# A channel stage in two passes, token mixing by split operands, and an order written as a list

## The chip, the cores and the metric

One core of a Trainium2 chip. Its engines run their own instruction queues in order: TensorE (PE) multiplies matrices into 8 PSUM banks, VectorE (DVE), ScalarE (ACT) and GpSimd (POOL) work on tiles of 128 partitions, and SyncE (SP) starts transfers. Engines wait for each other through semaphores. The metric is the device time of one execution in microseconds; smaller is better. A profiled execution also has a span, from its first instruction to its last.

## The reference

Three stages follow one another: a recurrent attention with gates (2 sequences, 8 heads, 768 steps, width 40), a causal attention with 4 experts of which each token takes 2, and a mixer, first over the tokens, then over the channels. All in float32.

```python
for t in range(S):                                   # first stage
    m_new = np.maximum(f_gate[:, :, t] + m, i_gate[:, :, t])
    f_stab = np.exp(f_gate[:, :, t] + m - m_new)
    i_stab = np.exp(i_gate[:, :, t] - m_new)
    C = f_stab * C + i_stab * einsum('bhd,bhe->bhde', vt, kt)
    n = f_stab * n + i_stab * kt
    y[:, :, t] = sigmoid(o_gate[:, :, t]) * (C q) / max(|n q|, 1)
...
for e in range(E):                                   # second stage, x = y, width 320
    a = softmax(causal(scale * (x @ wq[e]) @ (x @ wk[e]).T))
    out += weight_of_expert_e * (a @ (x @ wv[e]) @ wo[e])
...
xt = x.transpose(0, 2, 1)                            # third stage
h = np.maximum(xt @ w_tok1, 0.0) @ w_tok2            # 768 -> 256 -> 768
u = x + h.transpose(0, 2, 1)
h2 = np.maximum(u @ w_ch1, 0.0) @ w_ch2              # 320 -> 1536 -> 320
return u + h2
```

## The kernel before

**Tiles and stages.** The 2 x 768 tokens are 12 row chunks of 128, (b, i) with b the sequence and i from 0 to 5. The first stage goes chunk by chunk (the functions `m_...`, tiles `vs`, `w`, `e`, `cc`, `cb`, `dc`, `dn`, `x`): inside a chunk as an attention with decays, between chunks by a state `cc`. `p_qk`, `p_v` and `p_rank` make queries, keys, values and the choice of experts (`q`, `ks`, `vg`); `a_scores`, `a_unit`, `a_value`, `a_scale` and `a_tail` are the second attention (`am`, `atr`, `c`, `yh`), and `a_tail` (L1023) leaves its output, a product with `wo`, as rows `u`. `t_hidden` (L1056) and `t_mix` (L1078) mix the tokens: `t_hidden` needs all six chunks of a sequence and gives `ht`, `t_mix` adds to `u`, chunk by chunk. `c_turn` (L1100) transposes u to `ut`, `c_hidden` (L1118) and `c_out` (L1135) are the channel products, `c_store` (L1150) adds the result to u and stores it.

**Precision.** Most products are split: an operand is a hi tile in the type fp32r and a lo tile, the rest; a product is hi·hi + hi·lo + lo·hi, three matmuls. The first token product is the exception: one matmul in fp32 per chunk and half, with the weight `tw` and the rows `u` unsplit (L1062).

**Weights of the mixer** come as 64-bit words and are turned into float32 by `narrow` (L543): ACT scales the upper halves (L556), DVE shifts (L559), puts the lower halves' bits in (L561), and the sign (L564), ACT makes hi (L571), DVE or POOL lo (L302). This is called conversion below. The channel weights are 12 blocks k (`cw`), each with a first (`c1`, 384 columns) and a second part (`c2`, 320). A block needs a home in SBUF: three have their own, others get what the first two stages leave, and the last five (`PAGED`) take large buffers.

**Channel stage.** For each of three groups g of four chunks, all 12 blocks are gone through: `c_hidden(k, g)` gives h (ACT hi, DVE lo L1131), `c_out(k, g)` adds into four PSUM banks, which stay taken over the 12 blocks. Then `c_store` adds each to u, on DVE, and stores.

**Order.** The engines' queues are filled by `Plan` (L81). Each part of the work is a generator, whose steps name the engines that may run them (A, V, G for ACT, DVE, POOL; W is DVE for a step that is not planned beside one of POOL), an assumed cost, what must be done first, and the buffers taken. The planner takes, step by step, what can start first by its assumed times (`LAG`, costs), ties going by `RANK`, and gives the step to the engine that it thinks earliest. Where PE would be idle, it puts filler matmuls on a constant tile (`fillers`, L307, tile `still`) until 46 us of planned time.

Of the kernel before, what the change touches and what calls it, by code (L numbers as in the profile page):

```python
# [12 lines left out]
F32 = mybir.dt.float32  # L13
# [21 lines left out]
PAGED = 5  # L35
# [5 lines left out]
FILL = 46.0  # L41
LAG = {f: {"P": p, "A": a, "V": v, "G": g, "S": x} for f, p, a, v, g, x in (
    ("P", 0.0, 0.2, 0.2, 0.24, 0.2), ("A", 0.17, 0.0, 0.12, 0.155, 0.15), ("V", 0.17, 0.12, 0.0, 0.155, 0.15),
    ("G", 0.13, 0.09, 0.09, 0.0, 0.12), ("S", 0.1, 0.1, 0.1, 0.1, 0.0), ("", 0.0, 0.0, 0.0, 0.0, 0.0))}
DEP = 0.115
TURN = 0.11
WINDOW = 3.4133
WARM = 6.85
ARRIVE = 1.7
RATE = 405.0  # L50
LATE = (11.0, 1.7), (22.0, 2.4), (0, 0.8)
DEEP = 8
COSTLY = {"V": 1.2, "G": 1.2}
PAT = {"P": 0.004, "A": 0.004, "V": 0.004, "G": 0.004, "S": 0.004}


RANK = [
# [23 lines left out]
class Plan:  # L81


    def __init__(self, free, pool, lands, fill):
        self.free = dict(free)
        self.pool = {t: [(0.0, "")] * n for t, n in pool.items()}
        self.events, self.counts = {}, {}
        self.live, self.waiting = [], {}
        self.now, self.eng, self.order = 0.0, "", 0
        self.mode, self.act, self.win, self.cold = "F", {}, 0, False  # L90
        self.port = 0.0
        self.lands = list(lands)
        self.fill, self.filling = fill, True

    def add(self, part):
        self.order += 1
        p = [(RANK[self.order - 1], self.order), part, None, 0.0, ""]
        self.resume(p)

    def resume(self, p):  # L100
        try:
            p[2] = next(p[1])
        except StopIteration:
            return
        self.park(p)

    def park(self, p):
        for k in p[2][1]:
            if k not in self.events:
                self.waiting.setdefault(k, []).append(p)  # L110
                return
        self.live.append(p)

    def mark(self, key, lag=0.0):
        self.events[key] = (self.now + lag, self.eng if not lag else "")
        for p in self.waiting.pop(key, []):
            self.park(p)
# [9 lines left out]
    def give(self, tag, n=1, lag=0.0):  # L127
        self.pool.setdefault(tag, []).extend([(self.now + lag, self.eng)] * n)

    def landed(self, kb):  # L130

        t = max(self.lands[-1], self.now + ARRIVE) + kb / RATE
        self.lands.append(t)
        return t + next(x for z, x in LATE if t < z or z == 0) * (kb > 100 or t < LATE[1][0]) - self.now

    def start(self, p):
        opts, after, take, keep, mode, _, dmas = p[2]
        deps = [(p[3], p[4])] + [self.events[k] for k in after]
        for tag, n in take:
            have = self.pool.get(tag, [])  # L140
            if len(have) < n + (keep.get(tag, 0) if isinstance(keep, dict) else keep):
                return None
            deps += sorted(have)[:n]
        best = None
        for o, cost in opts:
            e = "V" if o == "W" else o
            s = max([self.free[e], self.port if o in "WG" else 0.0] + [t + (LAG[f][e] if f != e else 0.0 if e in "PS" else DEP) for t, f in deps])
            if dmas:
                s = max(s, self.lands[dmas - 1 - DEEP] - 0.65 * (dmas - 1))
            if e == "P" and mode != self.mode:  # L150
                s += TURN
            if best is None or s + cost * COSTLY.get(e, 1.0) < best[0] + best[2] * COSTLY.get(best[1], 1.0):
                best = (s, e, cost)
        return best

    def clock(self, t):

        while (self.win + 1) * WINDOW <= t:
            last, full = [self.act.get(w, 0.0) / WINDOW for w in (self.win - 1, self.win)]
            self.cold = full < 0.44 if self.cold else full < 0.36 and last < 0.45  # L160
            self.win += 1
        return 1.91 if self.cold or t < WARM else 1.0

    def stream(self, s, cost, duty):
        long = cost * self.clock(s)
        t, end = s, s + long
        while t < end - 1e-9:
            w = int(t / WINDOW + 1e-9)
            z = min(end, (w + 1) * WINDOW)
            self.act[w] = self.act.get(w, 0.0) + (z - t) / long * cost * duty  # L170
            t = z
        return long

    def still(self, s):

        if not self.filling:
            return
        if s > FILL:
            self.filling = False
            self.give("bank")  # L180
            return
        n = 0
        while self.free["P"] + 0.17 < s:
            self.free["P"] += self.stream(self.free["P"], 0.056, 0.95)
            n += 1
        if n:
            self.fill(n)

    def run(self):
        while self.live:  # L190
            cand = {}
            for p in self.live:
                c = self.start(p)
                if c:
                    cand.setdefault(c[1], []).append((c[0], p, c[2]))
            if not cand:
                raise RuntimeError("no part can go on: %s" % [(p[0], p[1].__name__, p[2]) for p in self.live])
            pick = None
            for e, cs in cand.items():
                s0 = min(c[0] for c in cs)  # L200
                c = min((c for c in cs if c[0] <= s0 + PAT[e]), key=lambda c: c[1][0])
                if c[0] > s0 + 0.004:
                    fits = [x for x in cs if x[0] + x[2] <= c[0] + 0.03]
                    c = min(fits, key=lambda c: c[1][0]) if fits else c
# [21 lines left out]
def on(opts, *after, take=(), keep=0, mode="F", duty=0.9, dmas=0):  # L226
    opts = (opts,) if isinstance(opts[0], str) else opts
    t = {}
    for x in take:
        t[x] = t.get(x, 0) + 1  # L230
# [1081 lines left out]
```

## Time and profile before

| what | value |
|---|---|
| median of 3 runs | 338.07 us (337.53 to 338.20) |
| the profiled execution | 338.06 us |
| its span | 336.3 us |
| busy: PE, DVE, ACT, POOL | 327.9, 232.5, 176.5, 37.2 us |
| chain that ended last | 69% PE, 24% DVE |
| granted TensorE clock | 1.00 |

The table is read from the bottom: the clock is at its full value throughout, so a matmul has the same price everywhere. PE's 97% is a share of the whole span, in which filler matmuls and stretches paced by other engines count as busy, so the chain says more: what ended last was PE in most of the span and DVE in a part. Where these parts lie is to be seen in the rows below.

### The profile page before, as it was taken

The page shows a single profiled execution, that of the slowest core. Times are in us where ns is not written, and L with a number is a line of the kernel's source. Part 1 is how long each engine was busy: PE and PEld are TensorE (multiplying, and loading weights), DVE is VectorE, ACT ScalarE, POOL GpSimd, SP SyncE. Part 2 cuts the span into 40 slices and gives each one's busy share as a digit, 9 for nine tenths or more (in the row PEclk, how much of TensorE's full clock was granted, in tenths as well). Part 3 has the DMA queues.
Part 4 walks back from the last instruction along what each step waited for, and adds up shares of the span by engine and source line. Part 5 has one row for each costly group of instructions (what it writes and reads, how often), then busy time and mean ns, then how long its engine had stood idle before and what let it go on. Part 6 is the DMA issues. An engine that isn't in the chain of part 4 may idle for free.

```text
span 336.3 us, 7705 instructions
## 1 busy us (share of the span) xinstructions
PE 327.9 (97%) x3049; PEld 293.6 (87%) x3049; DVE 232.5 (69%) x662; ACT 176.5 (52%) x435; POOL 37.2 (11%) x65
## 2 busy tenths in 40 slices
PE   7899999999999999999999999999999999999995
PEld 6689999898998889888888898999999889898985
DVE  5999999999999799999878656996231122411113
ACT  4785797848578779776876634453111121211110
POOL 4311133241212010010201100000000000000000
PEclk9999999999999999999999999999999999999999
DMA  7973443633500367010002502200020000200002
GB/s 215 415 287 102 161 164 116 239 106 106 176 29 2 119 182 253 12 64 24 2 0 89 173 0 88 86 1 3 0 78 2 0 2 0 78 2 0 0 2 78
DMA packets 10300, 29.05 MB, mean 86 GB/s; under 512 B 1272, under 2 KB 3224, under 8 KB 10264
## 3 DMA queue, kind: packets, MB, share of 16 engines
q1 hardware_dynamic: 10120, 28.54, 24.6%
q8 instruction: 24, 0.39, 0.5%
q14 instruction: 12, 0.10, 0.1%
q10 hardware_dynamic: 144, 0.02, 0.0%
HBM read 26.50 MB, written 1.97 MB: 85 GB/s over the span
## 4 chain that ended last, share of the span: by engine, by line
PE 69%; DVE 24%; ACT 3%; issue 2%; DMA 1%; SPq 0%; DVEq 0%; ACTq 0%
PE bank L278 63%; PE bank L976 3%; DVE am L959 2%; DVE tf L561 2%; DVE e L681 2%; DVE tf L564 2%; DVE cw L302 1%; DVE w L305 1%; DVE tf L559 1%; PE bank L719 1%; ACT am L965 1%; DVE xt L771 1%; DVE vs L305 1%; DVE c L1026 1%; DMA gt<-in_dram 1%
## 5 line engine op out<-in xcount | busy, mean ns | idle before, releaser
L1131 DVE SCALAR_TENSOR_TENSOR h<-bank,h 128x512 fp32r<-128x512 f32 x36 | 24.8, 690 | 75.2 <-ACT h L1129 75.2
L278 PE MATMUL bank<-ut,cw 128*128 128x512 f32 x288 | 70.9, 395 | 0.0
L278 PE MATMUL bank<-cw,h 128*128 128x320 f32 x432 | 68.0, 310 | 0.0
L1129 ACT ACTIVATE h<-bank 128x512 fp32r<-128x512 f32 x36 | 21.5, 597 | 86.1 <-PE bank L278 86.1
L278 PEld LDWEIGHTS bank<-cw,h 128*128 128x128 f32 x432 | 65.0, 188 | 1.7
L278 PEld LDWEIGHTS bank<-ut,cw 128*128 128x128 f32 x288 | 53.0, 188 | 10.8 <-issue 0.2
L965 ACT ACTIVATE am<-am,mn 128x128 f32<-128x128 f32 (+5 forms) x48 | 32.1, 670 | 9.1 <-DVE mn L962 5.0
L959 DVE CUSTOM_DVE_ANT_0 am<-bank,mk 128x384 f32<-128x384 f32 (+3 forms) x64 | 30.5, 498 | 3.2 <-PE bank L278 2.8
L278 PE MATMUL bank<-xt,wh 128*128 128x256 f32 x144 | 25.7, 286 | 0.4 <-DVE e L681 0.4
L976 PE MATMUL bank<-ident,am 128*128 128x128 f32 x168 | 23.4, 275 | 0.3 <-ACT dn L746 0.2
L278 PEld LDWEIGHTS bank<-xt,wh 128*128 128x128 f32 x144 | 21.4, 188 | 1.3 <-DVE e L681 0.6
L299 ACT COPY atr<-bank 128x384 f32<-128x384 f32 (+3 forms) x51 | 20.7, 453 | 2.1 <-PE bank L976 1.7
L278 PE MATMUL bank<-atr,vg 128*64 128x128 f32 x336 | 21.6, 277 | 0.0
L556 ACT ACTIVATE tf<-raw 128x384 f32<-128x384 f32 (+1 forms) x32 | 17.2, 540 | 8.4 <-DVE cw L302 7.0
L976 PEld LDWEIGHTS bank<-ident,am 128*128 128x128 f32 x168 | 19.3, 140 | 2.3 <-ACT dn L746 0.5
L278 PE MATMUL bank<-ks,q 64*128 64x384 f32 (+2 forms) x192 | 20.9, 341 | 0.0
L278 PEld LDWEIGHTS bank<-atr,vg 128*64 128x64 f32 x336 | 18.3, 137 | 2.2 <-issue 0.4
L278 PEld LDWEIGHTS bank<-ks,q 64*128 64x128 f32 x192 | 15.2, 184 | 3.6 <-issue 1.2
L561 DVE SCALAR_TENSOR_TENSOR tf<-raw,tf 128x384 uint32<-128x384 uint32 (+1 forms) x32 | 16.6, 526 | 0.3
L564 DVE SCALAR_TENSOR_TENSOR tf<-raw,minus,tf 128x384 uint32<-128x384 uint32 (+1 forms) x28 | 16.1, 582 | 0.2
L681 DVE TENSOR_TENSOR e<-bank,e 128x512 f32<-128x512 f32 x24 | 16.0, 678 | 0.0
L571 ACT CAST cw<-tf 128x320 fp32r<-128x320 f32 (+1 forms) x24 | 11.7, 486 | 8.0 <-DVE tf L564 7.9
(165 smaller groups left out, 582.2 us busy)
## 6 DMA issues: line engine op xcount, KB each, us to landing
kv<-in_dram SPq DMA_DIRECT2D x11, 848.0 KB
raw<-in_dram SPq DMA_DIRECT2D x20, 384.0 KB
raw<-in_dram SPq DMA_DIRECT2D x13, 320.0 KB
os<-in_dram SPq DMA_DIRECT2D x4, 480.0 KB
out_dram<-u SPq DMA_DIRECT2D x12, 160.0 KB
raw<-in_dram SPq DMA_DIRECT2D x3, 386.0 KB
kv<-in_dram SPq DMA_DIRECT2D x1, 512.0 KB
gt<-in_dram SPq DMA_DIRECT2D x1, 512.0 KB
```

Of the source, the lines that this page charges most:

```text
L278: PE.matmul(o, lt, r, start=first, stop=last)
L299: (A.copy if e == "A" else V.tensor_copy)(o, i)
L556: A.activation(t, w[:, :, 1].bitcast(F32), AF.Copy, scale=2.0 ** -112)
L561: V.scalar_tensor_tensor(u, w[:, :, 0], 29, u, op0=OP.logical_shift_right, op1=OP.bitwise_or)
L564: V.scalar_tensor_tensor((hi if lo is None else t).bitcast(U32), w[:, :, 1], minus.bitcast(U32), u, op0=OP.bitwise_and, op1=OP.bitwise_or)
L571: A.copy(hi, t)
L681: V.tensor_mul(EE[n, u], PS[n][u], EE[n, u])
L959: V.tensor_tensor_reduce(a[:, b0 * 128:b1 * 128], s["p", e, ci], mks, -0.125, 3e38, OP.add, OP.min, s["mn"][:, ci, e:e + 1])
L965: A.activation(a[:, 0:w], a[:, 0:w], AF.Exp, bias=s["mn"][:, z, e:e + 1], scale=-1.0, accum_out=s["sm"][:, 0, e:e + 1])
L976: PE.transpose(pt[:, k - b0], a[:, k * 128:(k + 1) * 128], ident)
L1129: A.activation(h[0], p1, AF.Relu)
L1131: V.scalar_tensor_tensor(h[1], p1, 0.0, f32(h[0]), op0=OP.max, op1=OP.subtract)
```

## The change

**Order.** The planner goes: `ORDER` lists every step, x // 5 being the part and x % 5 the engine ("PAVGS"); a negative number is so many fillers (80 in all, 119 before), and `STOP` gives their bank back. Costs and keeps disappear from the code.

**Engines.** Several steps lose the choice of POOL: the w product of `m_carry`, the lo parts of the weights of the second attention and of wo, of the converted weights, the gates, the output gate's scaling.

**Token mixing.** `tw(0)` is split like the other weights, `a_tail` makes hi and lo tiles `up` of its output, and `t_hidden` has three matmuls per chunk and half.

**Channel stage.** Two passes h of six blocks each, and in each pass the three groups. Results are added to u after each pass, and stored after the second. Blocks of the first pass give their homes back when all three groups have used them (`room`); no block takes large buffers.

```diff
-PAGED = 5
+HALF = NK // 2
...
+        for x in ORDER:
+            if x == STOP:
+                self.give("bank")
+            elif x < 0:
+                self.fill(-x)
+            else:
+                self.step(self.parts[x // 5], "PAVGS"[x % 5])
...
     def m_carry(n):
...
-        yield on((pool(512), dve2(512)), ("kv", n))
+        yield on("V", ("kv", n))
         mul(plan.eng, w, w, KQ[n % KVB][:, 4:8])
...
     def out_weights():
...
-        yield on((dve2(640), pool(640)))
+        yield on("V")
         sub(plan.eng, WO[1], raw, f32(WO[0]))
...
     def narrow(src, n, home, rem, after, done):
...
-        if lo is None:
-            give("tf")
-            count(done, 4)
-            return
-        yield on(act(n))
+        yield on("A")
         A.copy(hi, t)
-        yield on((("G", (0.2 if rem else 0.1) + n / 435.0), ("W", 0.73 if rem else dve2(n)[1])))
+        yield on("V")
...
     def token_home(n):
-        TW[n] = [big([128, 4, 384], F32R if n else F32, "tw") for _ in range(n + 1)]
+        TW[n] = [big([128, 4, 384], F32R, "tw") for _ in range(2)]
...
     def a_tail(b, i):
...
         copy(plan.eng, uo(b, i), px)
-        give("bank")
         mark(("u0", b, i))
+        yield on("AV", take=["big"] * (1 - i % 2))
+        if i % 2 == 0:
+            UP[b, i // 2] = big([128, 2, 2, DM], F32R, "up")
+        hi, lo = [UP[b, i // 2][:, x, i % 2] for x in range(2)]
+        copy(plan.eng, hi, px)
+        yield on("V")
+        V.tensor_sub(lo, px, f32(hi))
+        give("bank")
+        mark(("up", b, i))
...
     def t_hidden(b, m):
...
-            mm(ph, tw(0, 0)[:, m0:m0 + 128], uo(b, c), c == 0, c == NCH - 1)
+            for k, (w, x) in enumerate(((0, 0), (0, 1), (1, 0))):
+                mm(ph, tw(0, w)[:, m0:m0 + 128], UP[b, c // 2][:, x, c % 2], c + k == 0, c == NCH - 1 and k == 2)
...
     def c_out(k, g):
         for i in range(4):
+            new = k % HALF == 0
...
+            if new and i == 0:
+                ACC[k // HALF, g] = [bank([128, DM]) for _ in range(4)]
...
+            if (k + 1) % HALF == 0:
+                mark(("done", k // HALF, 4 * g + i))
...
+        if k < HALF:
+            plan.tally(("cwused", k), 3, lambda: room(*HOME[k]))
...
+    def c_store(h, n):
+        yield on("V", ("done", h, n), *((("sp", n),) if h else ()))
+        V.tensor_add(uo(b, i), ACC[h, n // 4][n % 4], uo(b, i))
+        give("bank")
+        if h == 0:
+            mark(("sp", n))
+            return
...
+    for h in range(2):
+        for g in range(3):
+            for k in range(h * HALF, h * HALF + HALF):
+                add(c_hidden(k, g))
+                add(c_out(k, g))
+            for i in range(4):
+                add(c_store(h, 4 * g + i))
```

What the list moves is seen in the engines' queues; here three places of them. First POOL, from its first row of real work in the first stage on; before:

```order
L305 TENSOR_TENSOR vs<-kv_72,e 128x164
L297 TENSOR_SCALAR dc<-w 128x4
L305 TENSOR_TENSOR w<-w,kv_73 128x512
L305 TENSOR_TENSOR vs<-kv_74,e 128x164
L297 TENSOR_SCALAR dc<-w 128x4
L305 TENSOR_TENSOR cc_122<-cc_123,dc 128x164
L302 TENSOR_TENSOR wo_132<-raw,wo_131 128x640
```

and POOL at the same place in the new kernel:

```order
L222 TENSOR_TENSOR vs<-kv_72,e 128x164
L222 TENSOR_TENSOR vs<-kv_73,e 128x164
L222 TENSOR_TENSOR cc_123<-cc_122,dc 128x164
L222 TENSOR_TENSOR x<-os,dn 128x320
L222 TENSOR_TENSOR vs<-kv_74,e 128x164
L214 TENSOR_SCALAR rem<-x 128x128
L222 TENSOR_TENSOR vs<-kv_74,e 128x164
```

The 512 and 640 columns wide operations have left the queue, and more operations of 128 to 320 columns are in it.

Second PE where the first chunk of the second sequence comes to its product with wo (tiles `wo_131` hi, `wo_132` lo); before:

```order
L278 MATMUL bank<-ht,tw 128x320 x6
L1001 MATMUL bank<-ident,c 128x128 x2
L278 MATMUL bank<-ht,tw 128x320 x18
L278 MATMUL bank<-wo_131,yh 128x320
L278 MATMUL bank<-wo_132,yh 128x320
L278 MATMUL bank<-wo_131,yh 128x320 x2
L278 MATMUL bank<-wo_132,yh 128x320
L278 MATMUL bank<-wo_131,yh 128x320
```

and PE there in the new kernel:

```order
L881 MATMUL bank<-ident,am 128x128 x4
L195 MATMUL bank<-wo_131,yh 128x320
L195 MATMUL bank<-wo_132,yh 128x320
L195 MATMUL bank<-wo_131,yh 128x320 x2
L195 MATMUL bank<-wo_132,yh 128x320
L195 MATMUL bank<-wo_131,yh 128x320
L195 MATMUL bank<-atr,vg 64x128 x8
L195 MATMUL bank<-ks,q 128x384 x12
L195 MATMUL bank<-ht,tw 128x320 x6
```

All six mixing products of the first sequence (`ht,tw`, six matmuls each) now stand behind the wo product. Up to that product DVE has 444 instructions before and 416 after.

Third DVE in the channel stage. Before, the last conversions stand ahead of the eighth h of 36; from the seventh on:

```order
L1131 SCALAR_TENSOR_TENSOR h_3637<-bank,h_3636 128x512
L302 TENSOR_TENSOR cw<-tf,cw 128x256
L302 TENSOR_TENSOR cw<-tf,cw 64x128
L561 SCALAR_TENSOR_TENSOR tf<-raw,tf 128x320
L299 COPY rem<-u 128x128
L1131 SCALAR_TENSOR_TENSOR h_3657<-bank,h_3656 128x512
L1112 TENSOR_TENSOR ut<-bank,ut 128x3x128
L564 SCALAR_TENSOR_TENSOR tf<-raw,minus,tf 128x320
L302 TENSOR_TENSOR cw<-tf,cw 128x320
```

In the new kernel they reach to the 24th h; these stand from the 18th, the last of the first pass, to the 20th:

```order
L1046 SCALAR_TENSOR_TENSOR h_3951<-bank,h_3950 128x512
L1070 TENSOR_TENSOR u<-bank,u 128x320
L474 SCALAR_TENSOR_TENSOR tf<-raw,tf 128x320
L219 TENSOR_TENSOR cw<-tf,cw 128x320
L477 SCALAR_TENSOR_TENSOR tf<-raw,minus,tf 128x320
L472 TENSOR_SCALAR tf<-tf 128x384
L474 SCALAR_TENSOR_TENSOR tf<-raw,tf 128x384
L219 TENSOR_TENSOR cw<-tf,cw 128x320
L1070 TENSOR_TENSOR u<-bank,u 128x320
L1046 SCALAR_TENSOR_TENSOR h_3998<-bank,h_3997 128x512
```

The conversions of the last blocks have moved from the first third of the stage into its middle, among the additions of the first pass to u (L1070).

## Rows read from the trace of the kernel before

**Rows 1.** The page: span, and the chain that ended last by engine.

```profile
span 336.3 us, 7705 instructions
...
PE 69%; DVE 24%; ACT 3%; issue 2%; DMA 1%; SPq 0%; DVEq 0%; ACTq 0%
```

**Rows 2.** Busy time by stretch: length, each engine's busy us (instructions), clock, DMA share, GB/s.

```profile
10.00:155.00 145.00, 142.40 (x1810) 128.20 (x1809) 139.16 (x429) 108.83 (x288) 28.86 (x41) 1.00 0.41 144
155.00:193.00 38.00, 38.00 (x375) 32.48 (x375) 31.04 (x105) 27.62 (x68) 4.25 (x7) 1.00 0.18 58
193.00:230.00 37.00, 37.00 (x217) 33.41 (x214) 28.62 (x67) 17.05 (x37) 0.00 (x0) 1.00 0.13 40
230.00:332.00 102.00, 102.00 (x573) 92.31 (x572) 25.83 (x43) 17.97 (x32) 0.00 (x0) 1.00 0.04 14
```

**Rows 3.** The chain of waits, 150 to 172 us: start, us, what.

```profile
150.71 0.08 issue
...
152.07 0.40 DVE u L1088
...
154.46 0.86 PE bank L278 x4
```

**Rows 4.** The timeline of PE at two places: start us, us, engine, line, operation.

```profile
116.20 4.47 PE L278 MATMUL bank<-u,tw 128*128 128x320 f32 x16
120.50 0.38 PE L1001 MATMUL bank<-ident,c 128*128 128x128 f32 x2
...
211.71 2.78 PE L278 MATMUL bank<-ht,tw 128*128 128x320 f32 x18
214.33 2.02 PE L278 MATMUL bank<-ut,cw 128*128 128x512 f32 x8
```

**Rows 5.** The timeline of POOL and DVE where long operations of both meet.

```profile
14.31 1.76 POOL L305 TENSOR_TENSOR w<-w,kv 128x512 f32<-128x512 f32 x1 [1.87 <-DMA kv<-in_dram]
15.33 0.77 DVE L748 TENSOR_SCALAR dn<-dn 128x8 f32<-128x8 f32 x1
...
25.34 1.54 POOL L302 TENSOR_TENSOR wo<-raw,wo 128x640 fp32r<-128x640 f32 x1
25.48 1.95 DVE L305 TENSOR_TENSOR w<-w,kv 128x512 f32<-128x512 f32 x1
...
58.62 0.72 POOL L305 TENSOR_TENSOR x<-os,dn 128x320 f32<-128x320 f32 x1 [1.79 <-DVE dn L749]
59.01 0.88 DVE L305 TENSOR_TENSOR w<-w,kv 128x512 f32<-128x512 f32 x1
```

**Rows 6.** Tiles w, dn, tf: ns least/median/most, first and last start, forms.

```profile
L305 DVE TENSOR_TENSOR w<-w,kv x9: 676/693/1950, 25.5 to 96.2; 128x512 f32<-128x512 f32 x9
...
L748 DVE TENSOR_SCALAR dn<-dn x12: 141/164/767, 15.3 to 109.7; 128x8 f32<-128x8 f32 x12
...
L302 DVE TENSOR_TENSOR cw<-tf,cw x33: 289/418/493, 117.6 to 230.1; 128x320 fp32r<-128x320 f32 x11, 128x256 fp32r<-128x256 f32 x11, 64x128 fp32r<-64x128 f32 x11
...
L559 DVE TENSOR_SCALAR tf<-tf x32: 313/352/792, 44.7 to 225.8; 128x384 uint32<-128x384 uint32 x20, 128x320 uint32<-128x320 uint32 x12
L561 DVE SCALAR_TENSOR_TENSOR tf<-raw,tf x32: 477/546/560, 45.6 to 227.4; 128x384 uint32<-128x384 uint32 x20, 128x320 uint32<-128x320 uint32 x12
L564 DVE SCALAR_TENSOR_TENSOR tf<-raw,minus,tf x28: 537/606/621, 84.7 to 229.0; 128x384 uint32<-128x384 uint32 x16, 128x320 uint32<-128x320 uint32 x12
```

**Rows 7.** Groups by line and shape: busy us, mean ns of one, idle before.

```profile
L1131 DVE SCALAR_TENSOR_TENSOR h<-bank,h 128x512 fp32r<-128x512 f32 x36 | 24.8, 690 | 75.2 <-ACT h L1129 75.2
...
L1088 DVE TENSOR_TENSOR u<-bank,u 128x320 f32<-128x320 f32 x12 | 5.8, 480 | 0.0
...
L305 DVE TENSOR_TENSOR vs<-kv,e 128x164 f32<-128x164 f32 x13 | 4.6, 366 | 0.0
...
L299 DVE COPY rem<-x 128x128 f32<-128x128 f32 x6 | 1.4, 235 | 0.0
...
L495 DVE TENSOR_SCALAR os<-os 128x960 f32<-128x960 f32 x1 | 0.9, 921 | 0.0
```

More of the change, by code (lines that the diff above doesn't have):

```diff
@@ L40, with __init__, mark @@
 EARLY = 4
[L41 to L57, printed above, removed]
[20 rows of a table removed]
+STOP = -1000
+ORDER = [
[11 rows of a table added]
+    937, 422, 524, 895, 187, 508, 432, 900, STOP, 560, 917, 187, 440, 488, 936, 896, 387, 440, 561, 901, 1482, 530,
[67 rows of a table added]
 ]
 class Plan:
[L84 to L93, printed above, removed]
-    def add(self, part):
[L96 to L103, printed above, removed]
-            return
[L105 to L117, printed above, removed]
+    def __init__(self, pool, fill):
+        self.pool, self.fill = dict(pool), fill
+        self.events, self.counts, self.parts = set(), {}, []
+        self.eng = ""
+    def add(self, part):
+        self.parts.append([part, next(part)])
+    def mark(self, key):
+        self.events.add(key)
     def tally(self, key, total, then):
@@ L125, in count @@
         self.tally(key, total, lambda: self.mark(key))
[L127 to L187, printed above, removed]
-    def run(self):
[L190 to L204, printed above, removed]
-                if pick is None or c[0] < pick[1][0]:
-                    pick = (e, c)
-            e, (s, p, cost) = pick
-            for tag, n in p[2][2]:
-                have = sorted(self.pool[tag])
-                self.pool[tag] = have[n:]
-            if e == "P":
-                self.still(s)
-                self.mode = p[2][4]
-                cost = self.stream(s, cost, p[2][5])
-            self.free[e] = self.now = s + cost
-            self.eng = e
-            if e == "G" or e == "V" and any(o == "W" for o, _ in p[2][0]):
-                self.port = self.now
-            p[3], p[4] = self.now, e
-            self.live.remove(p)
-            self.resume(p)
-        if self.waiting:
-            raise RuntimeError("parts wait for %s" % list(self.waiting))
@@ L226, in on @@
[L226 to L230, printed above, removed]
-    return opts, after, list(t.items()), keep, mode, duty, dmas
-def act(n):
-    return "A", 0.06 + n / 1150.0
-def dve(n):
-    return "V", 0.07 + n / 960.0
-def dve2(n):
-    return "W", 0.08 + n / 960.0
-def pool(n):
-    return "G", 0.1 + n / 435.0
-def pool1(n):
-    return "G", 0.16 + n / 840.0
-def pe(n, cols):
-    return "P", n * max(cols / 2400.0 + 0.0135, 0.11)
@@ L258, in scan, with give, step @@
-def scan(n):
-    return "W", 0.15 + n / 480.0
+    def give(self, tag, n=1):
+        self.pool[tag] = self.pool.get(tag, 0) + n
+    def step(self, part, eng):
+        engines, after, take = part[1]
+        if eng not in engines or not self.events.issuperset(after):
+            raise RuntimeError("%s is not ready on %s" % (part[0].__name__, eng))
+        for tag in take:
+            self.pool[tag] = self.pool.get(tag, 0) - 1
+            if self.pool[tag] < 0:
+                raise RuntimeError("%s finds no %s" % (part[0].__name__, tag))
+        self.eng = eng
+        part[1] = next(part[0], None)
@@ L262, in fused_kernel, with on @@
+    def run(self):
+        for x in ORDER:
[5 more added lines that the diff above has]
+                self.step(self.parts[x // 5], "PAVGS"[x % 5])
+        if any(p[1] for p in self.parts):
+            raise RuntimeError("parts are left over")
+def on(engines, *after, take=()):
+    return engines, after, take
 @with_exitstack
@@ L830, in last @@
             for t in ("wl", "wh"):
-                home(*two(wts.tile([128, 2, 704], F32R, name="cw", tag=t)))
+                room(wts, t)
         plan.tally(("xused", b, st), 4, then)
@@ L881, in p_rank @@
         n = c1 - c0
-        yield on(("W", 0.58 if n > 2 else 0.42), *[("v", b, c) for c in range(c0, c1)], take=["g"])
+        yield on("V", *[("v", b, c) for c in range(c0, c1)], take=["g"])
         lg = VG[b][:, c0:c1, 256:260]
@@ L924, in a_scores @@
             wm = max(wc, 256)
-            yield on(("P", wm / 800.0 + 0.09), ("q", b, st), *[("k", b, x) for x in range(st + 1)],
-                     *((("sc", n - 1, len(cuts(i if j else (i - 1) % NCH)) - 1),) if n else ()), take=["bank"] * 2 + first, mode="H")
+            yield on("P", ("q", b, st), *[("k", b, x) for x in range(st + 1)], *((("sc", n - 1, len(cuts(i if j else (i - 1) % NCH)) - 1),) if n else ()), take=["bank"] * 2 + first)
             if j == 0 and ci == 0:
@@ L1102, in c_turn @@
         g, n = divmod(b * NCH + i, 4)
[L1103 removed]
+        yield on("AVG", ("u", b, i), ("utal", g), take=["rem"])
         rem = twice(uo(b, i))
[L1105 removed]
+        yield on("P", take=["bank"])
         pu = bank([128, 3, 128])
```

274 lines of the change are left out of this document (125 added, 149 removed), and 98 rows, old and new, of tables (ORDER, RANK).

## The prediction

> **What bounds the kernel now.** I read the span and the summary of the chain of waits first, then the busy time by stretch, then the chain around the place where its engine changes, and last the groups that the change touches. The span is 336.3 us, and the chain that ends last lies on TensorE (PE) for 69% of it and on VectorE (DVE) for 24% [rows 1]; 1.76 us of the profiled 338.06 lie outside the span, and that execution is within 0.01 us of the median. The stretches say where each counts [rows 2]. From 155 us on PE has no idle time at all (38.00 of 38, 37.00 of 37, 102.00 of 102). From 10 to 155 us DVE is busy for 139.16 of 145 us, idle for 5.84; PE is busy for 142.40 there, filler matmuls among them, and much of that is a PE whose pace DVE sets. [...]
>
> The chain of waits shows the hand-over [rows 3]: it runs through DVE until 154.46 us and then enters PE at the product of the attention output with wo, of the first chunk of the second sequence. So I cut there: time = when DVE has issued what stands ahead of that product (154.46) + what PE does from it to the end (336.3 − 154.5 = 181.9, no waits) + 1.76. An edit counts if it changes DVE's work ahead of the cut or PE's work behind it.
>
> **Token mixing by split operands.** One fp32 matmul per row chunk and half becomes three fp32r ones. The trace shows each fp32 matmul as two records: 16 of `u,tw` start at 116.20 us and the next group at 120.50, .269 us each; 18 of `ht,tw`, already fp32r with the same 320 columns, take from 211.71 to 214.33, .146 each [rows 4]. So 2 × .269 = .54 us becomes 3 × .146 = .44. [...]
>
> Behind the cut PE gains the second mixing product of the first sequence, which stood ahead of it before (36 × .146 = +5.26), and the second sequence's first product changes from 24 records (−6.46) to 36 (+5.26): **+4.1 us**. Ahead of the cut PE loses 6.5 us by the same prices, so it doesn't take DVE's place there.
>
> The split costs DVE: the attention output (128x320 out of a bank) gets a hi copy and a lo subtraction; 6 lo and 2 hi stand on DVE ahead of the cut, at .480 as the addition of the same shape (L1088) [rows 7]: 3.84. Four more subtractions of the token weights, 128x384, at the .546 of a DVE operation of that shape (L561 [rows 6]): 2.18. Sum **+6.0**. The bank of the output stays taken until the lo subtraction has ended, by two operations longer; next to the 8 banks I put that at nothing. The 39 fillers that fall away (of 119) ran where PE waited for DVE, and cost nothing either.
>
> **Long GpSimd operations on DVE.** Ahead of the cut DVE gains one w product (.676 to .693 [rows 6]) and the wo subtraction, 128x640, bounded by that and by the .921 of a 128x960 operation [rows 7]; I take .8, near the middle in size: **+1.5**. In return their hold on DVE goes: w stood on DVE for 1.95 us while GpSimd made wo (25.34 to 26.88), and dn for .77 while GpSimd made its w (14.31 to 16.07) [rows 5], against least times of .676 and .141 [rows 6]. **−1.9**, both on the chain.
>
> **The fixed list.** The order of the changed kernel on DVE has 416 instructions ahead of the cut, where there were 444. Beside the above:
> - Evacuations that ScalarE had: 5 of 512 columns, 7 of about 320. No row has the cast itself on DVE; the nearest are .480 (320 columns) and .690 (h, 512 columns) [rows 7]. I take .6 and .48: **+6.4** (5.8 to 6.8).
> - 21 short operations go to GpSimd: 6 rem at .235 and 15 vs, yh, c, cc, x between .366 and .480 [rows 7], say .39: **−7.2**.
> - 12 go to ScalarE (cb, rt, os, mc, xt) at .235 to .921 [rows 7], .45 on average: **−5.4**.
> - 5 additions of u (.48), 3 lo of q and k (.68) and 12 operations of the channel weights' conversion (3 × .352, 3 × .546, 2 × .606, four subtractions at .29 to .42 [rows 6]) now stand behind the cut, where DVE is busy for 31.04 of 38 and 28.62 of 37 us [rows 2]: **−9.7**.
>
> The net is 6.0 + 1.5 + 6.4 − 7.2 − 5.4 − 9.7 = −8.4. Durations overlap: L1088 lasts .480, yet the chain counts .40 for it [rows 3, 7]. For 28 instructions fewer I give back 28 × .08 = 2.2: **−6.2**.
>
> GpSimd was busy for 28.86 of 145 us [rows 2], so 21 short operations don't make it a bound. They can hold DVE as the long ones did: beside GpSimd's x (58.62 to 59.34) a DVE w took .88 [rows 5], .2 over its least time. Long ones off and short ones on, there are about 13 more; if half of them meet a DVE operation, at .2 each, **+1.3**. The ends are 0 and 13 × .72 (x's whole length) = 9.4.
>
> **The channel stage in two passes.** PE's products stay the same in number. Twelve more additions of u (12 × .48) fall where DVE is busy for 25.83 of 102 us [rows 2] and cost nothing. The last eight weight blocks are no longer needed in the first 12 steps, but the last four now wait for a home that the first four give back after their third row group. A conversion waits there for a home, and behind it on DVE's queue stands the h of the next step, for which PE waits. In the new order DVE has 46 instructions between the 16th and the 23rd h, with those conversions and five additions of u among them: 25 us by the means of rows 6 and 7, 21.5 less the overlap of .08 each. PE's seven steps of 20 matmuls, at 102/573 us each [rows 2], are 24.9 us. That is nearly level. I take **+.5**, ends 0 and 6.4 (rival C). Where PE still waits for DVE after the cut, in the scores of the next chunks, I add **+.4** from the .08 of issue that the chain shows between two DVE steps [rows 3], five times.
>
> **Sum.** Cut: −6.2 + 4.1 = −2.1. Holds −1.9, added short ones +1.3, later points +.4, second pass +.5: −1.8. Hence 338.06 − 1.8 = **336.2 us** (336.26, and the profiled execution equals the median). Its own range is 333.8 (evacuations at their low end −.6, no hold by the short ones −1.3, no wait in the second pass −.5) to 337.4, where faster ends.
>
> **Rivals.**
> *A, more is won.* Of DVE's 5.84 idle us between 10 and 155 half, 3.0, is filled with work that stood later: 333.2. For: the steps on which DVE waits can now stand anywhere in a list; against: DVE is already 96% busy [rows 2].
> *B, no change.* Evacuation and subtraction now alternate between DVE and ScalarE more often; two more hand-overs for each of 12 chunks at the .08 of issue [rows 3] to .1 give 2.3: 338.5. For: PE was 142.40 of 145 busy ahead of the cut, so little slack may be there; against: PE's share there falls too.
> *C, slower: the second pass starves.* If the last four blocks can't be converted as fast as PE takes them, each step costs DVE 4.2 (two conversions of .352 + .546 + .606, and three subtractions between .289 and .493, 1.2 together [rows 6]) + .69 (h) + .42 (its share of additions) against PE's 3.6: some 1.6 short, over four blocks 6.4, where the sum has .5: 342.1. It decides if the conversions can't start before the home is free and DVE has no lead of a block by then. Against: their home is free seven steps ahead.
> *D, slower: each added short GpSimd operation holds DVE whole.* By that, 9.4 in place of 1.3: 344.3; with half the length 339.6. The .88 of w speaks for .2, the 1.95 beside wo for the whole [rows 5]. [...]
>
> **How the numbers follow.** Likeliest 336.2: .46. A .16, B .14 with D by half .05, C .09, D whole .04, others .06 (.04 of them slower). A measurement tells .2% = .68 us from no change, 337.4 to 338.7. Faster: .46 + .16 + .02 = .64; same: B and half of D's half, .17; slower: the rest, .19. The range begins at 331.9 (A, with the 1.3 of the short ones gone) and ends at 340.8 (B, with the 13 short ones at .28 each in place of .1, 2.3 more); C, D whole and the others, about .19, are left out.
>
> **What would show it.** In the profile after: `u,tw` gone and 72 of `up,tw` at .146 apart; the hand-over from DVE to PE nearly 7 us earlier (−6.2 − 1.9 + 1.3), near 148 us, with 4 us more PE work behind it; no w over .9 and no dn over .3; PE without idle time from there on, also where h of the second pass begins. Wrong would be: DVE idle for clearly more or less than 5.84 us ahead of the cut (B, A), PE idle before a hidden product of the last four blocks (C), many DVE operations longer by .3 and more beside GpSimd's (D), or a granted clock below 1.00, since 39 of the 119 fillers go.

## The result and the profile after

The changed kernel takes 334.22 us (median of 4, 333.95 to 334.47) where the kernel before takes 338.08: ratio .9889, 95% interval .9872 to .9906, 3.9 us faster. I had forecast 336.2, within 331.9 to 340.8: the range holds the result, but the gain is twice the 1.9 us that I forecast. The profiled execution after took 334.46, with a span of 332.7. Its page, the lines that answer to [rows 1], with the engines' busy time:

```profile
span 332.7 us, 7751 instructions
PE 326.1 (98%) x3034; PEld 293.8 (88%) x3034; DVE 243.1 (73%) x674; ACT 179.4 (54%) x453; POOL 43.3 (13%) x82
...
PE 57%; DVE 32%; ACT 4%; issue 3%; DMA 2%; SPq 0%; POOL 0%; DVEq 0%; POOLq 0%; ACTq 0%
```

DVE's share of the chain has grown from 24 to 32%. The forecast was made by a cut, so I read the new trace at it. The timeline of PE shows the wo product of the second sequence's first chunk:

```profile
145.52 1.13 PE L195 MATMUL bank<-wo,yh 128*128 128x320 f32 x6
```

In the kernel before this group starts at 153.87 and waits for its third matmul's operand until 154.46 [rows 3]; here it doesn't wait, so 145.52 answers to 154.46 within .3 us. The cuts of the experiments are starts of this group.

Busy time by stretch, as in [rows 2], ahead of and behind the cut; first the kernel before:

```profile
10.00:154.46 144.46, 141.86 (x1808) 127.66 (x1806) 138.62 (x427) 108.70 (x288) 28.86 (x41) 1.00 0.41 144
154.46:336.30 181.84, 178.41 (x1164) 159.34 (x1164) 87.41 (x219) 62.77 (x137) 4.25 (x7) 1.00 0.09 32
```

and the changed kernel:

```profile
10.00:145.52 135.52, 133.53 (x1731) 120.44 (x1732) 131.67 (x400) 105.70 (x286) 30.38 (x51) 1.00 0.41 145
145.52:332.70 187.18, 183.64 (x1217) 165.85 (x1215) 105.84 (x260) 66.25 (x150) 9.16 (x15) 1.00 0.11 36
...
193.00:230.00 37.00, 37.00 (x223) 34.34 (x223) 18.86 (x41) 8.74 (x20) 2.14 (x3) 1.00 0.06 21
230.00:328.00 98.00, 98.00 (x548) 88.59 (x548) 44.15 (x90) 24.57 (x47) 0.00 (x0) 1.00 0.09 29
```

The cut is reached 8.94 us earlier and 5.34 us more stand behind it: 3.6 us in the span. The 8.94 are 6.95 of DVE's busy time (138.62 to 131.67) and 1.99 of its idle time (144.46 − 138.62 = 5.84 to 135.52 − 131.67 = 3.85). PE lost 8.33 us of busy time ahead of the cut (about 2.8 of them filler matmuls) and has 2.0 idle there (2.6 before). Through the two passes PE has no idle time at all.

The prices of the new operations stand in the groups by line and shape and in two tiles' rows:

```profile
L958 DVE TENSOR_TENSOR up<-bank,up 128x320 fp32r<-128x320 f32 x12 | 5.7, 479 | 0.5 <-ACT up L216 0.5
L219 DVE TENSOR_TENSOR tw<-tf,tw 128x384 fp32r<-128x384 f32 x8 | 4.3, 539 | 0.0
L216 DVE CAST q<-bank 128x512 fp32r<-128x512 f32 x3 | 2.0, 679 | 0.0
L219 DVE TENSOR_TENSOR wo<-raw,wo 128x640 fp32r<-128x640 f32 x1 | 1.0, 1005 | 0.0
...
L222 DVE TENSOR_TENSOR w<-w,kv x10: 681/684/887, 14.4 to 108.3; 128x512 f32<-128x512 f32 x10
L654 DVE TENSOR_SCALAR dn<-dn x12: 137/164/627, 16.9 to 114.0; 128x8 f32<-128x8 f32 x12
```

### The profile page after: what moved, and what is told of

The parts are those of the page before. It is cut to its first block, busy times and chain, and to the rows that moved or that the text cites. A ratio compares the mean times of both kernels' runs of the same rounds, so it can differ in the third digit from the quotient of the medians.

```text
span 332.7 us, 7751 instructions
## 1 busy us (share of the span) xinstructions
PE 326.1 (98%) x3034; PEld 293.8 (88%) x3034; DVE 243.1 (73%) x674; ACT 179.4 (54%) x453; POOL 43.3 (13%) x82
## 4 chain that ended last, share of the span: by engine, by line
PE 57%; DVE 32%; ACT 4%; issue 3%; DMA 2%; SPq 0%; POOL 0%; DVEq 0%; POOLq 0%; ACTq 0%
PE bank L195 52%; DVE am L864 3%; PE bank L881 3%; DVE e L587 3%; DVE tf L477 3%; DVE tf L474 2%; DMA gt<-in_dram 2%; DVE cw L219 1%; DVE w L222 1%; DVE tf L472 1%; DVE xt L677 1%; ACT am L870 1%; DVE x L222 1%; PE bank L625 1%; DVE q L763 1%
## 5 line engine op out<-in xcount | busy, mean ns | idle before, releaser
L195 PE MATMUL bank<-ut,cw 128*128 128x512 f32 x288 | 72.4, 395 | 0.0
L195 PE MATMUL bank<-cw,h 128*128 128x320 f32 x432 | 70.6, 310 | 0.0
L195 PEld LDWEIGHTS bank<-cw,h 128*128 128x128 f32 x432 | 66.0, 188 | 2.7 <-issue 0.2
L195 PE MATMUL bank<-xt,wh 128*128 128x256 f32 x144 | 26.6, 290 | 0.0
L881 PE MATMUL bank<-ident,am 128*128 128x128 f32 x168 | 24.8, 275 | 0.0
L195 PE MATMUL bank<-ks,q 64*128 64x384 f32 (+2 forms) x192 | 22.4, 343 | 1.1 <-DVE q L763 1.0
L216 ACT COPY atr<-bank 128x384 f32<-128x384 f32 (+3 forms) x53 | 22.2, 442 | 2.0 <-PE bank L881 1.9
L477 DVE SCALAR_TENSOR_TENSOR tf<-raw,minus,tf 128x384 uint32<-128x384 uint32 (+1 forms) x32 | 19.1, 595 | 0.2
L474 DVE SCALAR_TENSOR_TENSOR tf<-raw,tf 128x384 uint32<-128x384 uint32 (+1 forms) x32 | 17.5, 556 | 0.3
L1070 DVE TENSOR_TENSOR u<-bank,u 128x320 f32<-128x320 f32 x24 | 11.0, 486 | 8.5 <-PE bank L195 8.5
```

What stands on the lines that cost most here:

```text
L195: PE.matmul(o, lt, r, start=first, stop=last)
L216: (A.copy if e == "A" else V.tensor_copy)(o, i)
L474: V.scalar_tensor_tensor(u, w[:, :, 0], 29, u, op0=OP.logical_shift_right, op1=OP.bitwise_or)
L477: V.scalar_tensor_tensor(t.bitcast(U32), w[:, :, 1], minus.bitcast(U32), u, op0=OP.bitwise_and, op1=OP.bitwise_or)
L881: PE.transpose(pt[:, k - b0], a[:, k * 128:(k + 1) * 128], ident)
L1070: V.tensor_add(uo(b, i), ACC[h, n // 4][n % 4], uo(b, i))
```

## The experiments

Changes are to the changed kernel where nothing else is said. Times are medians, with the ratio to the kernel before on the same chip; the changed kernel stands at 334.22 and .9889.

**1. The split undone.** The freed steps stay in the list and issue nothing.

```diff
+        whole = home[:2] == ("tw", 0)
-        V.scalar_tensor_tensor(t.bitcast(U32), w[:, :, 1], minus.bitcast(U32), u, op0=OP.bitwise_and, op1=OP.bitwise_or)
+        V.scalar_tensor_tensor((hi if whole else t).bitcast(U32), w[:, :, 1], minus.bitcast(U32), u, op0=OP.bitwise_and, op1=OP.bitwise_or)
...
-        copy(plan.eng, hi, px)
         yield on("V")
-        V.tensor_sub(lo, px, f32(hi))
...
-            for k, (w, x) in enumerate(((0, 0), (0, 1), (1, 0))):
-                mm(ph, tw(0, w)[:, m0:m0 + 128], UP[b, c // 2][:, x, c % 2], c + k == 0, c == NCH - 1 and k == 2)
+            mm(ph, tw(0, 0)[:, m0:m0 + 128], uo(b, c), c == 0, c == NCH - 1)
```

> The changed kernel with one part undone: the first token product is fp32 again, so DVE and ScalarE make no hi and lo parts of the attention output and of the first token weights; the list of steps stays, the freed steps are empty. Theory (DVE's work ahead of the wo product of the second sequence's first chunk, the cut, sets the time; PE's work behind it adds): 12 to 13 DVE operations fewer ahead of the cut at .40 to .48, 5 to 6 us, and 12 products behind it at .54 in place of .44, +1.2: 334.2 - 5.5 + 1.2 = 330 (329.4 to 330.8). Rival (PE ahead of the cut paces too, and a fixed list leaves the freed DVE time idle): 334 to 336.6, the 24 products x .1 at most.

Measured: 334.32 us, .9903 (.9886 to .9919), the same as the changed kernel, as the rival has it; the theory's 330 is out. Taken as a whole the split is neither the gain nor a cost. Busy time from 10 us to its cut, at 144.65, and the chain by engine:

```profile
10.00:144.65 134.65, 133.18 (x1719) 119.20 (x1719) 127.34 (x389) 102.80 (x278) 30.45 (x51) 1.00 0.42 145
...
PE 82%; DVE 12%; DMA 2%; issue 1%; ACT 1%; SPq 0%; POOL 0%; DVEq 0%; POOLq 0%
```

DVE has 4.3 us less to do and is idle for 7.3 of 134.65; the cut moved by .87 only, for now PE is most of the chain, with 1.5 us idle. The run doesn't relieve DVE alone: by the expectation's prices the fp32 products give PE up to 1.2 us more ahead of the cut. Runs 9 and 11 leave PE's work as it is. Behind the cut it takes .47 longer (187.65 against 187.18), where the prediction had priced the split at 1.2 less there.

**2 to 4. Doses**, to measure what a microsecond of each engine is worth: DVE ahead of the cut, PE ahead of it, PE behind it.

```diff
-        V.tensor_sub(lo, pq, f32(hi))
+        for _ in range(2 - b):
+            V.tensor_sub(lo, pq, f32(hi))
...
-        V.tensor_sub(lo, px, f32(hi))
+        for _ in range(2 - b):
+            V.tensor_sub(lo, px, f32(hi))
```

For PE the six matmuls of the wo product stand in a loop, in run 4 with `range(1 + b)`:

```diff
-        k = 0
-        for j in range(2):
+        for _ in range(2 - b):
+            k = 0
+            for j in range(2):
```

> The changed kernel with 12 DVE operations more ahead of the cut: in the first sequence the lo part of the attention output (6 x .40 of chain time) and of queries and keys (6 x .60) is made twice. Theory (DVE sets the time there): the whole 6.0 us, 340.2 (339.2 to 341.2). Rival (DVE's 3.85 idle us ahead of the cut take it up, or PE paces): 336 or less.

> The changed kernel with PE's product with wo made twice for the six chunks of the first sequence, 36 matmuls x .146 = 5.2 us, all ahead of the cut. Theory (DVE sets the time there, PE has slack): 0 to 1.5 us more, 334.2 to 335.7. Rival (PE is a second bound there): most of 5.2, 338 to 339.4.

> The changed kernel with the same product made twice for the six chunks of the second sequence, 5.2 us of PE from the cut on. Theory (PE without slack behind the cut): 5.2 us more, 339.4 (338.7 to 339.8). Rival (the chain still goes through DVE and ScalarE for 20 us behind the cut, so that PE has slack there): 336 to 338.

Measured: DVE ahead +5.1 of 6.0 us (339.33; 1.0045, 1.0032 to 1.0058), PE ahead +3.5 of 5.2 (337.75; .9992, .9983 to 1.0002), PE behind +4.5 of 5.2 (338.75; 1.0028, 1.0018 to 1.0038). Runs 2 and 4 fall in their theory's range. Run 3 is out of both: more than the theory's 1.5, a little less than the rival's 3.8. A microsecond more, as priced, costs .85 on DVE and .68 on PE ahead of the cut: two bounds, not one. The traces show what the doses really added; DVE's first, up to its cut at 150.40, then PE's up to 149.11:

```profile
10.00:150.40 140.40, 136.12 (x1731) 121.08 (x1731) 136.81 (x412) 105.63 (x286) 29.94 (x51) 1.00 0.40 138
...
10.00:149.11 139.11, 137.82 (x1766) 125.67 (x1767) 132.30 (x400) 106.26 (x286) 30.48 (x51) 1.00 0.41 141
```

DVE was busy for 5.14 us more and the cut came 4.88 later; PE was busy for 4.29 more and the cut came 3.59 later. PE's dose also raised DVE's idle time ahead of the cut from 3.85 to 6.81 us: a good part of DVE's idle time there is waiting for PE. And it turned the chain as the undone split did:

```profile
PE 73%; DVE 17%; ACT 3%; DMA 3%; issue 2%; SPq 1%; POOL 0%; DVEq 0%; POOLq 0%; ACTq 0%
```

**5. Two long operations back on GpSimd.** The names of the two steps allow it again, and two entries of the list change from V to G.

```diff
+for p in (63, 217,):
+    ORDER[p] += 1
...
-        yield on("V", ("kv", n))
+        yield on("VG", ("kv", n))
```

> The changed kernel with two long operations given back to GpSimd, at their places in the list: the first w product (128x512) and the lo part of wo (128x640). Theory (a long GpSimd operation holds a DVE one that meets it, 1.27 and .63 us in the kernel before, where DVE saves .6 and .9): within .2 to .4 us of the changed kernel, 334.6 (334.0 to 335.2). Rival 1 (no hold, DVE's work alone counts): 332.7. Rival 2 (each holds DVE for its whole length, 1.76 + 1.54, less what DVE saves): 336.0.

Measured: 334.75, .9902 (.9888 to .9916): +.5 by the medians, within the intervals' width, in the theory's range. The timeline of POOL and DVE shows what each met:

```profile
14.84 1.50 POOL L225 TENSOR_TENSOR w<-w,kv 128x512 f32<-128x512 f32 x1 [1.56 <-ACT dc L219]
15.29 1.32 DVE L222 TENSOR_TENSOR gt<-gt 128x256 f32<-128x256 f32 x1
...
38.56 1.28 DVE L590 TENSOR_TENSOR e<-bank,e 128x512 f32<-128x512 f32 x2
38.89 1.55 POOL L222 TENSOR_TENSOR wo<-raw,wo 128x640 fp32r<-128x640 f32 x1
```

The subtraction on `gt`, .42 in the changed kernel, stood for 1.32 until GpSimd's w was over (16.34) and .27 more. Two products `e` beside GpSimd's wo took .64 each, as in the changed kernel, and were not held. So the theory's .63 for the hold by wo did not come; the total fits all the same.

**6. Short operations back on DVE.**

```diff
+for p in (32, 46, 94, 118, 126, 128, 180, 199, 261, 284, 306, 463, 559, 572,):
+    ORDER[p] += -1
```

> The changed kernel with all 14 short vs operations of GpSimd on DVE, at their places in the list. Theory (a short GpSimd operation holds DVE for .1 on average): DVE has 14 x (.366 - .08) = 4.0 us more and loses 1.4 of holds: 336.8 (336.0 to 337.8). Rival (each holds DVE for its whole .52 us): 14 x .52 = 7.3 less, 4.0 more: 330.9.

Measured: 335.34, .9925 (.9913 to .9936), +1.1: slower as the theory has it, but below its range, by less than half of its size, and far from the 330.9 of whole holds. Rival D falls with it. DVE's busy time ahead of the cut (146.47 here) rose by 1.39 only, 131.67 to 133.06, where 14 operations of .32, less .08 of overlap each, would be 3.4; by this estimate 2.0 of holds went, .14 each. Moving these 14 off DVE brought about 1 us.

**7. All parts but the list**, by the planner of the kernel before, with its ranks.

```diff
+                plan.order = base + 28 * g + 2 * k
+                add(c_hidden(k, g))
+                add(c_out(k, g))
...
+        copy(plan.eng, hi, px)
+        yield on(dve(320))
+        V.tensor_sub(lo, px, f32(hi))
```

> All parts of the change but the list: two passes, split token product, no long work on GpSimd, with the planner of the kernel before setting the order. It gives DVE 465 instructions ahead of the cut (444 in the kernel before, 416 in the changed one). Theory (DVE's count ahead of the cut sets the time; the gain comes with the list, which moved short work off DVE and conversions behind the cut): 338.1 + 21 x .4 - 1.9 of holds + 1 of PE less behind the cut = 343 (341 to 345). Rival (the list brought only the 2 us less of DVE's idle time): 336.2.

Measured: 380.33, 1.1218 (1.1171 to 1.1264). Slower as the theory said, but by 46 us more than the changed kernel and not by the mechanism given. The longest wait of PE (line waited for, us in total, times, the longest), and some stretches in the columns of [rows 2]:

```profile
PE bank L970 <- ACT am L959: 12.0, 2, 11.2
...
76.00:80.00 4.00, 2.39 (x46) 2.04 (x44) 3.76 (x16) 1.07 (x4) 0.00 (x0) 1.00 0.00 0
80.00:84.00 4.00, 3.31 (x54) 2.91 (x53) 3.94 (x9) 1.88 (x5) 0.46 (x1) 0.65 0.02 4
84.00:88.00 4.00, 4.00 (x24) 2.99 (x22) 1.79 (x7) 1.92 (x5) 1.34 (x2) 0.50 0.02 4
...
172.00:176.00 4.00, 2.37 (x14) 1.39 (x14) 3.88 (x15) 2.65 (x10) 0.00 (x0) 0.50 0.00 0
```

PE waited 11.2 us at one place (162 to 174 us, where the chain goes through DVE's conversions and the choice of experts), and the granted clock was .50 in two parts of the trace: from 84 to 96 us, after PE had been busy for 5.70 of the 8 us before, and from 168 to 180 us, in this wait and after it. Over the whole span PE is idle for 27.2 us (6.6 in the changed kernel) and busy for 25.8 more, at the clock of .50 in these parts and with 219 fillers in place of 80. The parts and an order for them can't be separated here: this planner's order for these parts starves PE. It says that the parts need another order, not what the list is worth.

**8. The two passes alone**, in the kernel before, with the same planner.

```diff
-    for g in range(3):
-        for k in range(NK):
+    for h in range(2):
+        for g in range(3):
+            for k in range(h * HALF, h * HALF + HALF):
...
+        if k < HALF:
+            plan.tally(("cwused", k), 3, lambda: room(*HOME[k]))
```

> The kernel before with the two passes of the channel stage alone, the planner setting the order; ahead of the cut the engines' queues are the same as before. Theory (the passes cost PE nothing and the 12 additions more lie under it; without other work ahead of the cut nothing is won): 338.1 (337.5 to 338.9). Rival C of the prediction (the last four blocks' conversions starve PE): up to 344.5.

Measured: 344.68, 1.021 (1.0191 to 1.0228), 6.7 slower. The theory's range (337.5 to 338.9) is missed. The size is near rival C's, the mechanism is not, so that the sizes agree is chance. Busy time by stretch, and the chain at the first change of group:

```profile
155.00:193.00 38.00, 36.16 (x328) 29.46 (x326) 33.39 (x112) 29.35 (x73) 3.21 (x5) 1.00 0.16 49
193.00:230.00 37.00, 35.73 (x237) 31.82 (x237) 15.48 (x34) 8.80 (x18) 0.00 (x0) 1.00 0.04 10
...
224.37 1.81 DVE u L1156 x4
226.18 0.14 DVE rem L299
...
226.37 0.34 PE bank L718
...
226.74 0.49 ACT ut L299
...
228.36 0.49 ACT ut L299
...
228.89 1.32 PE bank L278 x4
```

The conversions of the last blocks run between 250 and 290 us, where DVE is busy again and PE is never idle; the first hidden product starts at 195.81 us:

```profile
250.00:270.00 20.00, 20.00 (x112) 18.07 (x111) 12.02 (x27) 7.60 (x15) 0.00 (x0) 1.00 0.13 37
...
195.81 3.97 PE L278 MATMUL bank<-ut,cw 128*128 128x512 f32 x16
```

Time is lost earlier, at two places. From 155 to 193 us DVE is busy for 33.39 us (31.04 in [rows 2]) and ScalarE for 29.35 (27.62), and PE waits, longest, for 1.5 us, for ScalarE's `am`; this product comes 2.5 us later than in the kernel before (193.33). At the first group's end the planner put the four additions to u ahead of four turns, which then went one by one through PE, ScalarE and DVE (224.4 to 228.9). In the changed kernel the turns of the next group stand between earlier products, and PE has no gap.

**9 and 10. Less DVE, and less of both.** Without lo parts; in 10 the first sequence's product is also made once instead of three times.

```diff
-        sub(plan.eng, lo[:, 0:m], t[:, 0:m], f32(hi[:, 0:m]))
+        if home[:2] != ("tw", 0):
+            sub(plan.eng, lo[:, 0:m], t[:, 0:m], f32(hi[:, 0:m]))
...
-        V.tensor_sub(lo, px, f32(hi))
...
-            for k, (w, x) in enumerate(((0, 0), (0, 1), (1, 0))):
-                mm(ph, tw(0, w)[:, m0:m0 + 128], UP[b, c // 2][:, x, c % 2], c + k == 0, c == NCH - 1 and k == 2)
+            for k in range(3):
+                mm(ph, tw(0, 0)[:, m0:m0 + 128], UP[b, c // 2][:, 0, c % 2], c + k == 0, c == NCH - 1 and k == 2)
```

Run 10 has 2 b + 1 in place of the 3.

> The changed kernel without the lo parts of the attention output and of the first token weights; the first token product multiplies hi by hi three times instead, so PE has the same work and DVE 10 operations fewer ahead of the cut (6 + 4, some 4.5 us). The lo terms are left out. Theory 1 (DVE alone sets the time ahead of the cut): 334.2 - 4.5 = 329.7 (329 to 330.6). Theory 2 (after the undone split brought nothing: DVE and PE are both nearly full there, 3.85 and 2.0 us idle of 135.5, so taking from one alone uncovers the other): 333.0 (332.2 to 334.2).

> As e9, with hi by hi multiplied only once for the first sequence: besides DVE, PE has 24 matmuls x .146 = 3.5 us less ahead of the cut, nothing less behind it. The lo terms are left out. Theory 1: as e9, 329.7. Theory 2: both engines have less, so the time falls by most of the 3.5: 330.4 (329.4 to 331.8), at least 1.5 below e9. Theory 3 (hand-overs between engines set the time there, not an engine's work): as the changed kernel, 333.5 to 334.5 in both.

Measured: 332.56 (.9852, .9831 to .9872) and 331.71 (.9822, .9808 to .9836). The first lies in theory 2's range, 1.7 us below the changed kernel by the medians and 1.2 by the ratios. The second lies at the upper edge of theory 2's range, but only .9 below the first, not 1.5 and more. Busy time of 10 up to its cut, at 143.78:

```profile
10.00:143.78 133.78, 130.32 (x1709) 117.24 (x1708) 127.90 (x390) 105.59 (x286) 30.45 (x51) 1.00 0.42 147
```

PE is idle for 3.5 and DVE for 5.9 us: with both relieved neither is full. Of PE's idle time 3.2 us are four single waits, two for DVE (`q` .9, `c` .8) and two for ScalarE (`vg` 1.0, `e` .5). That is theory 3's mechanism for this part, though its range (333.5 to 334.5) is missed; that these waits set the time is not shown. Some of the gain isn't ahead of the cut at all: behind it run 9 takes 186.42 us and run 10 186.62, where the changed kernel takes 187.18.

**11. The evacuations back on ScalarE.**

```diff
+for p in (166, 230, 287, 356, 417, 456, 547, 548, 604, 605, 624, 661, 714, 721, 772, 859,):
+    ORDER[p] += -1
```

> The changed kernel with the 16 evacuations ahead of the cut that the list moved from ScalarE to DVE back on ScalarE, at their places in the list. Theory 1 (DVE alone): 16 x .43 = 6.9 less: 327.3. Theory 2 (PE is nearly full too): 333.2 (332.4 to 334.4). Theory 3 (ScalarE, busy for 106 of 135.5 us there, becomes late): 335 to 337.

Measured: 334.39, .9904 (.9890 to .9918), no change; theory 1's 327.3 is out, and the result lies at the upper end of theory 2's range (332.4 to 334.4). By the counts of the two traces, 12 of the 16 are those of the prediction's sum, two are hi copies that the split brought, and two were on DVE in the kernel before too. Busy time to its cut, at 145.46:

```profile
10.00:145.46 135.46, 133.84 (x1730) 120.36 (x1729) 125.02 (x384) 110.48 (x302) 30.33 (x51) 1.00 0.42 144
```

DVE has 6.65 us less to do, all of it idle now (10.4), and the cut stands where it stood. PE is idle for 1.6 and makes up 72% of the chain, ScalarE 5%, which speaks for PE and against a late ScalarE as what holds the cut there.

**12. Less PE in the kernel before.**

```diff
-            for w, x in ((0, 0), (1, 0), (0, 1)):
+            for w, x in ((0, 0), (1, 0), (0, 1)) if b else ((0, 0),):
```

> The kernel before with two of the six matmuls of each second token product of the first sequence: PE has 24 x .146 = 3.5 us less, most of it ahead of the cut, the engines' order is the same. The lo terms of that product are left out. Theory 1 (DVE alone sets the time ahead of the cut in the kernel before): 337.5 to 338.1. Theory 2 (PE, idle for 2.6 us there against DVE's 5.8, is a bound there as well): 336.3 (335.4 to 337.2).

Measured: 339.51, 1.0052 (1.0038 to 1.0066): slower, which neither theory had. The cut stands at 153.40, .5 us earlier than the start of that group in the kernel before (153.87), and .3 of it were there at the first wo product; so 3.5 us of PE bought next to nothing ahead of the cut. The 24 matmuls stood between 146.9 and 153.9 us: in this last stretch ahead of the cut PE's work didn't set the time in the kernel before. Of the stretch before it this run says nothing. Time by stretch around the cut:

```profile
148.00:151.00 3.00, 2.19 (x13) 1.43 (x11) 2.92 (x11) 1.79 (x6) 0.61 (x1) 1.00 0.70 240
151.00:154.00 3.00, 0.56 (x2) 0.30 (x2) 3.00 (x9) 1.05 (x3) 0.00 (x0) 1.00 0.02 5
154.00:157.00 3.00, 2.92 (x22) 2.40 (x22) 2.87 (x8) 1.86 (x6) 0.00 (x0) 0.66 0.00 0
157.00:160.00 3.00, 3.00 (x19) 2.48 (x17) 2.44 (x9) 1.83 (x5) 0.00 (x0) 0.77 0.00 0
```

PE was busy for 2.75 of 6 us, and then the granted clock was .66 and .77: 16 matmuls of `atr,vg` took 1.98 us from 155.11 on, and 16 of the same shape 1.09 from 171.98 on. If PE's work goes with the clock, 6 us at .71 lose 1.7 us of it, an estimate; the part behind the cut is 1.57 longer (184.00 against 182.43), so this is most likely the loss. All five executions show it, with a mean granted clock of .988 to .995.

## Why the prediction was right, and where its steps were wrong

**The cut and its total held.** DVE's busy time ahead of the cut fell by 6.95 us where the sum had 6.8 (6.2 + 1.9 − 1.3), and 5.3 us came behind it where the sum had 4.1 and .9. (336.3 − 154.5 is 181.8 and not 181.9; nothing hangs on it.) The 5.3 are made otherwise than the sum said, and that their total agrees is partly luck: PE's busy time behind the cut rose by 5.2 (178.41 to 183.64), its idle time by .1 only, where .9 had been taken for waits. The split of the second sequence's product saved less there than the 1.2 of the sum, .5 by run 1.

**That DVE alone bounds the kernel ahead of the cut was too much.** Its 24% of the chain are 81 us of the 144 [rows 1], so PE had much of the rest, before the change too. Run 12 shows for the last 7 us ahead of the cut that PE's work wasn't the bound; no run takes work from DVE alone in the kernel before.

**The size was half, because the sum took DVE's idle time as fixed.** It fell from 5.84 to 3.85, 2.0 us, with the cut at 145.5 instead of 147.7. In size that is near rival A, which had 3.0 and a chance of .16: a term for it belonged into the forecast. A's mechanism, later work that the list moves into the gaps, no run shows alone. Run 3 points to another: with 5.2 us of work given back to PE, DVE's idle time is 6.81, more than before the change. That speaks for PE's smaller load as at least a part of it.

**"PE loses 6.5 us as well, so it doesn't take DVE's place there" was the weak step.** PE lost 8.3 us of busy time ahead of the cut. That was needed, not a footnote: PE had 2.6 us idle there, and for a cut 8.9 us earlier at least 6.3 had to leave PE too. About 2.8 of the 8.3 are fillers. In the changed kernel both are within 2 to 4 us of full. Each term taken alone therefore is worth other than the sum said: the split's +6.0 on DVE is worth nothing (run 1), the 16 evacuations nothing (run 11; the sum had +6.4 for 12 of them), ten lo operations of some 4.5 us 1.2 to 1.7 with what came behind the cut (run 9), the 14 short operations 1.1 (run 6). Taking from one engine uncovers the other, and adding to either costs .7 to .85 of each microsecond priced.

**Single prices.** The up and tw operations cost .479 and .539 (.480 and .546 taken), the 512-column evacuations .68 (.6 taken, inside its bounds), the wo subtraction 1.005, above the .921 taken as its upper end. No w over .9 came true (.887), no dn over .3 did not (.627, beside GpSimd's `e`, an operation that the kernel before has too). Short GpSimd operations hold DVE now and then, as the +1.3 had it: run 6 gives 2.0 for 14 by an estimate.

**The second pass cost nothing, .5 was taken.** PE stays full. But that is the order's doing: by another order the passes cost 6.7 us (run 8). That this is close to rival C's 6.4 is chance: it came from the turns and additions at the change of group and from a later start of the stage, not from late conversions. The mechanism was looked for at the wrong place.

**The hand-over "near 148" after which PE never waits was wrong in form.** The chain after runs through DVE until 164.6 us, with PE busy beside it:

```profile
164.17 0.41 DVE u L1002
164.58 0.04 issue
164.63 1.42 PE bank L195 x17
```

PE was idle for .12 us only from the cut to 165, so "never waits" nearly held, but PE's work wasn't what set the time there. So PE work behind the cut is worth .87 on average (4.5 of 5.2, run 4) and not 1: the doubled products, .87 us each, delayed what follows by .47, .67 and .49 in the first three chunks and by .83 and more from the fourth on.

What stays open: what the list alone is worth, since run 7 gave the other parts an order that starves PE. Undone one by one, the long operations are worth .5 at most, the 14 short ones 1.1 and the split nothing; that the rest of the 3.9 comes from the order is by exclusion, and such terms need not add up where two engines are nearly full. And why the freed time of runs 9 and 10 is only partly won: the profiled execution of run 9 (333.83) is the slowest of its four, so its trace can't place the gain.

## What to carry to other kernels

Before pricing an edit by the engine on the chain, look how full the second engine is in the same stretch: with PE idle for 2 us of 135, 4 to 7 us taken from DVE were worth between nothing and 1.7, where the change took 7 and 8 us from both and won 3.9. Make a dose on each engine first: a few operations made twice, with the same result, told here what a microsecond costs, which the sum had wrong. Look in the trace at what a dose really added. A restructuring that adds changes of group must be priced at these changes with its order, since the same two passes left PE without a gap by one order and cost 6.7 us by another.

## What the runs showed of the hardware

- Work taken away made a kernel slower, 339.51 us at a ratio of 1.0052 (run 12): 3.3 us without PE work between 148 and 154 us were followed by a granted clock of .66 and .77, where the kernel before, with PE busy for all of these 6 us, has 1.00. In run 7 the clock was at .50 from 84 to 96 us, after PE had been busy for 2.39 and 3.31 of 4 us. Filler matmuls late in a kernel may thus be worth having; no run here tries it.
- Beside GpSimd's work some DVE operations took longer and others did not. In run 5 a subtraction of two SBUF tiles, .42 in the changed kernel, took 1.32 and ended .27 after GpSimd's w; products of a PSUM bank and an SBUF tile beside GpSimd's wo took their usual .64. An operation with one tile as input took longer too: dn, .77 beside GpSimd's w [rows 5], and .63 beside GpSimd's `e` in the changed kernel, where its median is .164. What decides it no run shows. In the prediction I counted all short GpSimd operations alike.
